# A written-out order for all five queues, new from the first gated attention to the first channel mixing

## The chip, the core and the metric

The kernel runs on one core of a Trainium2 chip. The metric is the device time of one launch in microseconds (us), lower is better; of several runs of one kernel the median counts. Five engines work in parallel, each through a queue of its own in the order in which the queue is written: PE (TensorE), DVE (VectorE), ACT (ScalarE), POOL (GpSimd) and SP (SyncE, which here only issues DMAs). An instruction that needs another engine's result waits on a semaphore, and all that stands behind it in the same queue waits too.

## What is computed

Three layers follow each other, on two batch entries of 768 positions:

```python
x = concat_heads(banded_attention(q, k, v))     # 8 heads of 64; 31-wide band and 24 block summaries
for e in range(4):                              # gated attention: 4 experts, the 2 best are weighted per position
    q, k, v = x @ wq[e], x @ wk[e], x @ wv[e]
    a = softmax(causal(q @ k.T / 8))
    out += gate[:, e] * (a @ v @ wo[e])
u = out + (relu(out.T @ w_tok1) @ w_tok2).T     # token mixing
y = u + relu(u @ w_ch1) @ w_ch2                 # channel mixing, 512 -> 1536 -> 512
```

The top-2 gate is a softmax over the two largest of four logits. The matrices of the mixings arrive as 64-bit floats and are decoded on the chip.

## The kernel before

Almost every product runs as three matmuls of the rounded fp32r type (`mm3`, lines 112 to 114): each operand is kept as a high part, which ACT writes, and a remainder, which DVE subtracts (`split`, lines 104 and 105), so each matmul result costs one ACT and one DVE pass before it can be multiplied again.

The stages, with the names that the rows use (b is the batch entry, e the expert, h the half of 384 positions):

- `s1`, the banded attention (lines 217 to 282); its tiles begin with s1, and sm, ri, pr.
- `proj`: pv (values and gate logits, b and block) and pj (queries and keys). Their split copies are moved by SP's DMAs into q2, k2 and k2l.
- `attn`, the gated attention: for each of 4 experts and 2 halves, PE makes the scores s2s (line 476: queries by keys, then by the keys' remainder) in a PSUM bank of the group "sc"; DVE masks and takes the row minimum of the negated scores (line 481, tiles pr and mn); ACT takes the exponential (line 486, which adds up sm); POOL adds a small constant (488); DVE inverts (489, tile f); POOL scales pr by f and the gate, three blocks of rows (492); PE turns pr in 128x128 blocks (502, bank s2p); ACT copies the turned block (104: ph, 506: pf), DVE makes the remainder (105: pl); PE multiplies by the values into s2a (507, 512, 513); ACT and DVE join the halves (516: tmp, 517: yT). The digits after s2s, s2p, s2a are b, e, h and then the bank. Half h = 0 has row blocks of 128, 256 and 384 keys, half h = 1 of 512, 640 and 768.
- `tokmix`, with tiles yh, yl, yt (turn, 535), nh, nl, z, g and u; `chmix`, with h and o, in four passes over 384 hidden columns.
- `decode_w` (lines 138 to 153): per 128x512 weights ACT 143 and 149, POOL 144, 150, 151 and 153, DVE 145 to 147, ACT 152. Tiles raw and deca; t1, t2, c1, c2 are the decoded weights.

The stages overlap: generators of the stages are interleaved by shares (`run`), so the first gated attention shares its time with `proj` of batch 1 and the decoding of the token weights, and the second with the token mixing of batch 0 and the first channel pass. `run` gives only the order in which the program is traced. What stands in the queues is chosen by the framework's scheduler from that, with its own estimates of durations; only the first banded attention (`FIRST`) is fixed by hand. PSUM has eight banks in three groups (sc 3, pt 3, acc 2), so a matmul that opens a bank also waits for the last reader of the bank's former tile.

Of the kernel before, what the change touches and what calls it, by code (L numbers as in the profile page):

```python
# [790 lines left out]
```

## Time and profile before

| | us |
|---|---|
| median of 3 runs | 466.64 |
| lowest, highest | 465.47, 469.15 |
| profiled execution, its own time | 467.73 |
| span of its instructions | 465.9 |
| PE busy in the span | 445.1 (96%) |

The rows further down come from the profiled execution. A row of the timeline gives the start (us from the span's start), the length, the engine, the line of the kernel, the operation, what it writes and reads, its shape, how many were merged, and in square brackets the idle time before it with the instruction that ended it. A PE matmul's length contains its way through the array, so neighbours overlap; what one costs is the distance to the next one's start.

### The profile page before, as it was taken

To read this page: it belongs to the slowest core of one execution; us is meant where nothing else is said; L and a number is where in the kernel's file an instruction comes from. 1 tells how busy PE (TensorE), PEld (TensorE's weight loads), DVE (VectorE), ACT (ScalarE), POOL (GpSimd) and SP (SyncE) were. 2 spreads that over 40 slices of the span, in tenths; PEclk is the share of its full clock that TensorE was granted. 3 is DMA by queue.
4 is the path that set the end of the run, shared out by engine and by line. 5 is a ranking of instruction groups with operands and counts; after the bars stand their busy time and mean duration, and the time that the engine had idled before them with its cause. 6 is when DMAs were issued, how large, how long until landed. Compare 5 with 4: busy or idle time off the path is not lost.

```text
span 465.9 us, 8565 instructions
## 1 busy us (share of the span) xinstructions
PE 445.1 (96%) x3038; PEld 420.7 (90%) x3038; DVE 280.1 (60%) x818; ACT 231.2 (50%) x653; POOL 285.2 (61%) x319
## 2 busy tenths in 40 slices
PE   7899899999989878999999999999999999999996
PEld 7798789989978766897999999999999999999996
DVE  5573766759699679868773743677572673332322
ACT  4685665977778687885664423233323321111010
POOL 4568542768989887997873869877864771000000
PEclk9999999999999999999999999999999999999999
DMA  7999917806515865021111120212121100001111
GB/s 222 275 255 310 289 39 207 182 2 167 127 46 152 210 171 146 3 91 45 45 47 46 66 70 2 84 53 78 58 91 45 62 32 0 1 0 69 68 70 68
DMA packets 28522, 46.51 MB, mean 100 GB/s; under 512 B 2496, under 2 KB 19648, under 8 KB 28480
## 3 DMA queue, kind: packets, MB, share of 16 engines
q1 hardware_dynamic: 28480, 45.97, 35.2%
q8 instruction: 24, 0.39, 0.4%
q14 instruction: 18, 0.15, 0.1%
HBM read 33.38 MB, written 3.15 MB: 78 GB/s over the span
## 4 chain that ended last, share of the span: by engine, by line
PE 68%; DMA 10%; DVE 7%; POOL 4%; ACT 3%; issue 3%; SPq 3%; DVEq 0%; ACTq 0%; POOLq 0%
PE h L113 7%; PE h L112 7%; PE h L114 7%; PE o L112 7%; PE o L113 7%; PE o L114 7%; DMA kx<-in_kwT_dram 5%; PE s1s L217 4%; PE s1a L271 2%; DMA qb<-in_qT_dram 2%; POOL pr L492 2%; PE u L112 2%; PE pj L112 2%; PE u L113 2%; PE u L114 2%
## 5 line engine op out<-in xcount | busy, mean ns | idle before, releaser
L144 POOL TENSOR_SCALAR deca<-deca 128x512 f32<-128x512 f32 x30 | 58.0, 1938 | 10.5 <-ACT deca L143 9.7
L113 PE MATMUL o<-hl,c2h 128*128 128x384 f32 x192 | 64.2, 337 | 0.0
L114 PE MATMUL o<-hh,c2l 128*128 128x384 f32 x192 | 64.0, 336 | 0.0
L108 ACT ACTIVATE hh<-h 128x384 fp32r<-128x384 f32 x48 | 23.3, 490 | 79.4 <-PE h L114 78.8
L109 DVE SCALAR_TENSOR_TENSOR hl<-h,hh 128x384 fp32r<-128x384 f32 x48 | 26.5, 555 | 53.2 <-ACT hh L108 53.2
L605 DVE TENSOR_TENSOR oa<-o,oa 128x384 f32<-128x384 f32 x64 | 31.9, 550 | 38.5 <-PE o L114 38.5
L112 PE MATMUL o<-hh,c2h 128*128 128x384 f32 x192 | 49.4, 336 | 0.0
L236 ACT ACTIVATE pr<-n,mn 128x120 f32<-128x120 f32 x96 | 36.6, 384 | 16.3 <-DVE mn L227 15.8
L150 POOL TENSOR_TENSOR raw<-raw 128x512 f32<-128x512 f32 x30 | 31.3, 1042 | 20.4 <-DVE raw L147 18.6
L492 POOL TENSOR_SCALAR pr<-pr,f,wg 128x128 f32<-128x128 f32 (+5 forms) x48 | 40.1, 849 | 5.1 <-DVE f L489 2.9
L151 POOL TENSOR_TENSOR deca<-deca,raw 128x512 f32<-128x512 f32 x30 | 40.8, 1360 | 1.0
L149 ACT ACTIVATE raw<-raw 128x512 f32<-128x512 uint32 x30 | 20.3, 677 | 36.3 <-DMA raw<-in_ch_dram 25.6
L145 DVE TENSOR_SCALAR deca<-deca 128x512 int32<-128x512 int32 x30 | 27.8, 928 | 14.9 <-POOL deca L144 14.9
L486 ACT ACTIVATE pr<-pr,mn 128x128 f32<-128x128 f32 (+5 forms) x48 | 31.9, 665 | 9.8 <-DVE mn L481 9.7
L113 PEld LDWEIGHTS o<-hl,c2h 128*128 128x128 f32 x192 | 36.0, 188 | 0.3 <-DVE hl L109 0.3
L114 PEld LDWEIGHTS o<-hh,c2l 128*128 128x128 f32 x192 | 36.0, 188 | 0.0
L112 PEld LDWEIGHTS o<-hh,c2h 128*128 128x128 f32 x192 | 34.8, 188 | 0.1
L113 PE MATMUL h<-u0l,c1h 128*128 128x384 f32 x96 | 32.5, 338 | 0.0
L112 PE MATMUL h<-u0h,c1h 128*128 128x384 f32 x96 | 32.4, 338 | 0.0
L114 PE MATMUL h<-u0h,c1l 128*128 128x384 f32 x96 | 32.3, 337 | 0.0
L112 PE MATMUL h<-u1h,c1h 128*128 128x384 f32 x96 | 32.3, 336 | 0.0
L113 PE MATMUL h<-u1l,c1h 128*128 128x384 f32 x96 | 32.3, 336 | 0.0
(207 smaller groups left out, 1315.1 us busy)
## 6 DMA issues: line engine op xcount, KB each, us to landing
raw<-in_ch_dram SPq DMA_DIRECT2D x24, 512.0 KB, 3.5
kx<-in_kwT_dram SPq DMA_DIRECT2D x7, 720.0 KB, 10.0
vx<-in_vw_dram SPq DMA_DIRECT2D x8, 576.0 KB, 11.1
qb<-in_qT_dram SPq DMA_DIRECT2D x16, 192.0 KB, 8.9
raw<-in_tok_dram SPq DMA_DIRECT2D x6, 512.0 KB, 4.6
out_dram<-oa SPq DMA_DIRECT2D x16, 192.0 KB, 2.0
vt<-in_vT_dram SPq DMA_DIRECT2D x4, 384.0 KB, 10.3
rqk<-in_wqkv_dram SPq DMA_DIRECT2D x4, 256.0 KB, 10.2
```

The lines of the kernel that those rows point to most:

```text
L109: vec.scalar_tensor_tensor(lo, src, 0.0, hi.bitcast(F32), op0=ALU.max, op1=ALU.subtract)
L112: ten.matmul(out, lh, rh, start=start, stop=False)
L113: ten.matmul(out, lh, rl, start=False, stop=False)
L114: ten.matmul(out, ll, rh, start=False, stop=stop)
L144: gps.tensor_scalar(af, af, F64_TINY, F64_HUGE, op0=ALU.max, op1=ALU.min)
L145: vec.tensor_scalar(ta, ta, 3, 0x3FFFFFFF, op0=ALU.logical_shift_left, op1=ALU.bitwise_and)
L150: gps.tensor_mul(lf, lf, ef)
L151: gps.tensor_add(af, af, lf)
L236: act.activation(pr[:, i, :], n[:, i, :], AF.Exp, bias=mn[:, i:i + 1], scale=-1.0, accum_out=sm[:, i:i + 1])
L486: act.activation(prs[r], prs[r], AF.Exp, bias=mn[:, r, ci:ci + 1], scale=-1.0, accum_out=sm[:, r:r + 1])
L492: gps.tensor_scalar(prs[r][:, :nk], prs[r][:, :nk], f[:, r:r + 1], wg[:, 3 * h + r, e:e + 1], op0=ALU.mult, op1=ALU.mult)
L605: vec.tensor_add(oa[d], a[:, :HALF], oa[d])
```

## The change

A table `ORDER` is added, with one line of positions for each of the five queues: it names, for each place in the queue, the traced instruction that stands there. At the end of the program a chain of dependencies without semaphores is laid along each line, so the scheduler has nothing left to choose:

```diff
+ORDER = {
+    "PE": """
+0-192 253-257 193-216 258-262 281-284 298 263-264 299-301 217-236 265 269-277 306-314 330-331 285 266 237-252 267-268
...
+    queues = {"PE": ten, "DVE": vec, "ACT": act, "POOL": gps, "SP": nc.sync}
+    traced = list(nc.cur_bb.bb.instructions)
+    for name, table in ORDER.items():
+        mine = [x for x in traced if x.engine == queues[name].engine and type(x).__name__.startswith("Inst")]
+        places = []
+        for run_ in table.split():
+            a, _, z = run_.partition("-")
+            places += range(int(a), int(z or a) + 1)
+        assert sorted(places) == list(range(len(mine))), (name, len(places), len(mine))
+        for a, z in zip(places, places[1:]):
+            tc.add_manual_dep(mine[z], mine[a].name, NOSYNC, reason="keep_in_program_order")
```

No instruction is added, dropped or resized. Ahead of the 506th PE instruction (88 us of the trace before) and from the 1742nd on (299 us) the queues are those of before. Between them other places hold 1138 of 2673 PE instructions, 352 of 818 on DVE, 251 of 508 on ACT, 128 of 315 on POOL and 29 of 142 DMA issues of SP. The table stands ahead of the code, so line numbers after the change are higher by 104 (L580 is L476 of before, L606 is L502, and so on).

**Place 1, ACT at the end of the first gated attention.** pf is the copy of a turned block that PE multiplies next; pf_2527 stands 14 rows behind pf_2500 in before. Its first rows (pr768_2633 is of batch 1, expert 0, second half; the pr of 2749 to 2751 of batch 1, expert 1, first half):

```order
L506 ACTIVATE pf_2500<-s2p0310_2496 128x384
L486 ACTIVATE pr768_2633,sm2_2629<-pr768_2633,mn2_2628 128x768
L104 ACTIVATE ph_2507<-s2p0311_2503 128x384
L486 ACTIVATE pr128_2749,sm2_2747<-pr128_2749,mn2_2746 128x128
L143 ACTIVATE deca_2734<-raw64_2733 128x512
L149 ACTIVATE raw64_2733<-raw64_2733 128x512
L486 ACTIVATE pr256_2750,sm2_2747<-pr256_2750,mn2_2746 128x256
L104 ACTIVATE s111h_2394<-pj1111_2439 128x384
L104 ACTIVATE ph_2517<-s2p0312_2513 128x384
L516 ACTIVATE tmp_2436<-s2a030_2411 64x384
L143 ACTIVATE deca_2813<-raw64_2812 128x512
L149 ACTIVATE raw64_2812<-raw64_2812 128x512
```

The rows from pf_2500 on now, where pf_2527 is nine rows behind it:

```order
L610 ACTIVATE pf_2500<-s2p0310_2496 128x384
L256 ACTIVATE t2h_2140<-deca_2273 128x2x256
L208 ACTIVATE ph_2507<-s2p0311_2503 128x384
L590 ACTIVATE pr256_2563,sm2_2560<-pr256_2563,mn2_2559 128x256
L590 ACTIVATE pr128_2562,sm2_2560<-pr128_2562,mn2_2559 128x128
L208 ACTIVATE s111h_2394<-pj1111_2439 128x384
L208 ACTIVATE ph_2517<-s2p0312_2513 128x384
L620 ACTIVATE tmp_2436<-s2a030_2411 64x384
L208 ACTIVATE yh0_2584<-yT0_1526 128x768
L610 ACTIVATE pf_2527<-s2p0313_2523 128x384
L208 ACTIVATE ph_2533<-s2p0314_2530 128x256
L208 ACTIVATE ph_2541<-s2p0315_2539 128x128
```

The two decoding pairs (deca and raw64) and the exponentials pr768_2633, pr128_2749, pr256_2750 and pr384_2751 of batch 1 stood between pf_2500 and pf_2527; now they stand behind pf_2527, and two exponentials of batch 1, expert 0, first half, are left between the two.

**Place 2, PE in the first gated attention, second half of expert 0.** Scores s2s011x of expert 1, and turns s2p001x of expert 0. Before:

```order
L502 MATMUL s2p0010_1750<-ident_76,pr512_1678 128x128
L502 MATMUL s2p0011_1757<-ident_76,pr512_1678 128x128
L502 MATMUL s2p0012_1767<-ident_76,pr512_1678 128x128
L476 MATMUL s2s0112_1929<-k200_1070,q200_1069 128x512
L476 MATMUL s2s0112_1929<-k2l00_1071,q200_1069 128x512
L502 MATMUL s2p0010_1750<-ident_76,pr640_1679 128x128
L502 MATMUL s2p0011_1757<-ident_76,pr640_1679 128x128
L502 MATMUL s2p0012_1767<-ident_76,pr640_1679 128x128
L476 MATMUL s2s0113_1934<-k200_1070,q200_1069 128x512
L476 MATMUL s2s0113_1934<-k2l00_1071,q200_1069 128x512
L502 MATMUL s2p0010_1750<-ident_76,pr768_1680 128x128
L502 MATMUL s2p0011_1757<-ident_76,pr768_1680 128x128
```

Now:

```order
L580 MATMUL s2s0112_1929<-k200_1070,q200_1069 128x512
L580 MATMUL s2s0112_1929<-k2l00_1071,q200_1069 128x512
L580 MATMUL s2s0113_1934<-k200_1070,q200_1069 128x512
L580 MATMUL s2s0113_1934<-k2l00_1071,q200_1069 128x512
L216 MATMUL pj1000_1968<-x1h0_717,wqk0h_111 128x384
L217 MATMUL pj1000_1968<-x1l0_719,wqk0h_111 128x384
L218 MATMUL pj1000_1968<-x1h0_717,wqk0l_112 128x384
L216 MATMUL pj1000_1968<-x1h0_717,wqk0h_111 128x384
L217 MATMUL pj1000_1968<-x1l0_719,wqk0h_111 128x384
L218 MATMUL pj1000_1968<-x1h0_717,wqk0l_112 128x384
L606 MATMUL s2p0010_1750<-ident_76,pr512_1678 128x128
L606 MATMUL s2p0010_1750<-ident_76,pr640_1679 128x128
```

The groups of three turns that stood between the score banks are taken out; the banks follow each other directly, then half of projection pj1000, and the turns come as nine in a row.

**Place 3, PE and DVE at the start of the second gated attention.** The last score bank of batch 1, expert 0, second half (s2s1013) and what follows it on PE. Before, where 75 instructions stand between it and the first turn of the same half, s2p1010:

```order
L476 MATMUL s2s1013_2651<-k210_1964,q210_1963 128x512
L476 MATMUL s2s1013_2651<-k2l10_1965,q210_1963 128x512
L513 MATMUL s2a021_2285<-pl_2332,V01_758 128x128
L502 MATMUL s2p0301_2419<-ident_76,pr256_2373 128x128
L502 MATMUL s2p0301_2419<-ident_76,pr384_2374 128x128
L535 MATMUL yt02_2724<-ident_76,yT0_1526 128x128
L507 MATMUL s2a030_2411<-pf_2416,V01_758 128x384
L502 MATMUL s2p0302_2428<-ident_76,pr384_2374 128x128
L502 MATMUL s2p0310_2496<-ident_76,pr512_2465 128x128
L502 MATMUL s2p0310_2496<-ident_76,pr640_2466 128x128
L502 MATMUL s2p0310_2496<-ident_76,pr768_2467 128x128
L512 MATMUL s2a030_2411<-ph_2422,V01_758 128x256
```

Now; behind the last row shown stand ten more instructions (one s2a031, one s2p1002, two s2s1101, two yt01, four s2a100), and then s2p1010:

```order
L580 MATMUL s2s1013_2651<-k210_1964,q210_1963 128x512
L580 MATMUL s2s1013_2651<-k2l10_1965,q210_1963 128x512
L606 MATMUL s2p1001_2601<-ident_76,pr256_2563 128x128
L606 MATMUL s2p1001_2601<-ident_76,pr384_2564 128x128
L617 MATMUL s2a031_2495<-pl_2534,V01_758 128x256
L616 MATMUL s2a031_2495<-ph_2541,V01_758 128x128
L639 MATMUL yt02_2724<-ident_76,yT0_1526 128x128 x2
L616 MATMUL s2a100_2590<-ph_2595,V10_1572 128x384
L580 MATMUL s2s1100_2752<-k210_1964,q210_1963 128x128
L580 MATMUL s2s1100_2752<-k2l10_1965,q210_1963 128x128
L580 MATMUL s2s1100_2752<-k210_1964,q210_1963 128x256
L580 MATMUL s2s1100_2752<-k2l10_1965,q210_1963 128x256
```

On DVE, from the last row minimum of the same half (pr768_2633) to the reciprocal f2_2630 that its scaling needs. Before:

```order
L481 ISA pr768_2633,mn2_2628<-s2s1013_2651,cmask_80,mn2_2628 128x512
L481 ISA mn2_2628 128x1
L517 TENSOR_TENSOR yT0_1526<-s2a021_2285,tmp_2337 64x384
L126 TENSOR_TENSOR wol_2341<-rw512_2346,woh_2340 128x512
L105 TENSOR_TENSOR pl_2423<-s2p0301_2419,ph_2422 128x256
L105 TENSOR_TENSOR pl_2431<-s2p0302_2428,ph_2430 128x128
L481 ISA pr128_2749,mn2_2746<-s2s1100_2752,cmask_80 128x128
L481 ISA mn2_2746 128x1
L481 ISA pr256_2750,mn2_2746<-s2s1100_2752,cmask_80 128x256
L481 ISA mn2_2746 128x1
L489 RECIPROCAL f2_2630<-sm2_2629 128x3
```

Now:

```order
L585 ISA pr768_2633,mn2_2628<-s2s1013_2651,cmask_80,mn2_2628 128x512
L585 ISA mn2_2628 128x1
L249 TENSOR_SCALAR deca_2734<-deca_2734 128x512
L209 TENSOR_TENSOR pl_2542<-s2p0315_2539,ph_2541 128x128
L230 TENSOR_TENSOR wol_2341<-rw512_2346,woh_2340 128x512
L585 ISA pr128_2749,mn2_2746<-s2s1100_2752,cmask_80 128x128
L585 ISA mn2_2746 128x1
L585 ISA pr256_2750,mn2_2746<-s2s1100_2752,cmask_80 128x256
L585 ISA mn2_2746 128x1
L250 SCALAR_TENSOR_TENSOR deca_2734<-raw64_2733,deca_2734 128x512
L593 RECIPROCAL f2_2630<-sm2_2629 128x3
```

Counted in PE instructions, s2s1013 has moved back by 47 places and s2p1010 has come forward by 7, so 21 instructions are left between the two. On DVE two steps of a weight's decoding (L249 and L250, of before L145 and L146) now stand between the row minimum and the reciprocal.

## Rows read from the trace of the kernel before

**Rows 1.** Windows: us, busy time (instructions) by engine, clock, DMA.

```profile
84.00:120.00 36.00, 36.00 (x325) 32.95 (x325) 25.25 (x108) 30.78 (x102) 27.55 (x45) 1.00 0.51 121
120.00:152.00 32.00, 30.14 (x186) 26.45 (x184) 27.17 (x86) 24.00 (x64) 29.64 (x31) 1.00 0.36 97
152.00:178.00 26.00, 22.07 (x131) 18.29 (x132) 19.82 (x55) 19.25 (x52) 21.69 (x25) 1.00 0.79 191
178.00:240.00 62.00, 58.47 (x359) 51.68 (x358) 50.19 (x127) 45.88 (x111) 53.39 (x50) 1.00 0.19 60
240.00:460.00 220.00, 220.00 (x1272) 219.14 (x1272) 103.86 (x172) 59.30 (x114) 107.26 (x82) 1.00 0.14 47
```

**Rows 2.** Waits of PE, 84 to 250 us: total, times, longest.

```profile
PE s2a L507 <- ACT pf L506: 1.8, 2, 1.3
...
PE s2s L476 <- DVE mn L481: 0.8, 2, 0.6
PE s2s L476 <- issue: 0.6, 1, 0.6
PE s2s L476 <- DMA k2l<-s101l: 0.6, 1, 0.6
...
PE yt L535 <- DVE yT L517: 0.3, 1, 0.3
```

**Rows 3.** Timeline of PE around one wait, 181.8 to 183.7 us.

```profile
181.89 0.42 PE L512 MATMUL s2a<-ph,V 128*128 128x384 f32 x1
183.17 0.38 PE L112 MATMUL z<-t1h,nh 128*128 128x256 f32 x1 [0.86 <-DVE mn L481]
183.40 0.28 PE L113 MATMUL z<-t1l,nh 128*128 128x256 f32 x1
```

**Rows 4.** Timeline of ACT, from pf_2500 to pf_2527 (place 1).

```profile
163.94 0.50 ACT L506 ACTIVATE pf<-s2p 128x384 f32<-128x384 f32 x1
...
167.14 0.70 ACT L143 ACTIVATE deca<-raw 128x512 f32<-128x512 f32 x1 [0.62 <-DMA raw<-in_ch_dram]
...
172.64 0.47 ACT L506 ACTIVATE pf<-s2p 128x384 f32<-128x384 f32 x1
```

**Rows 5.** Timeline of PE and DVE, 114.5 to 116.2 us (place 2).

```profile
114.54 0.69 DVE L481 CUSTOM_DVE_ANT_0 pr<-s2s,cmask 128x512 f32<-128x512 f32 x1 [0.68 <-PE s2s L476]
...
114.81 0.49 PE L502 MATMUL s2p<-ident,pr 128*128 128x128 f32 x3
...
115.30 0.50 PE L476 MATMUL s2s<-k,q 128*128 128x512 f32 x1
...
116.07 0.74 DVE L481 CUSTOM_DVE_ANT_0 pr<-s2s,cmask,mn 128x512 f32<-128x512 f32 x1
```

**Rows 6.** Timeline of four engines, 161.6 to 178 us: s2s1013 to s2p1010 (place 3).

```profile
161.64 0.40 PE L476 MATMUL s2s<-k2l,q 128*128 128x512 f32 x1
...
163.43 0.72 DVE L481 CUSTOM_DVE_ANT_0 pr<-s2s,cmask,mn 128x512 f32<-128x512 f32 x1
...
164.31 0.95 ACT L486 ACTIVATE pr<-pr,mn 128x768 f32<-128x768 f32 x1
...
166.38 0.20 POOL L488 TENSOR_SCALAR sm<-sm 128x3 f32<-128x3 f32 x1
...
166.61 0.18 DVE L489 RECIPROCAL f<-sm 128x3 f32<-128x3 f32 x1 [0.32 <-POOL sm L488]
...
166.96 2.60 POOL L492 TENSOR_SCALAR pr<-pr,f,wg 128x512 f32<-128x512 f32 x3 [0.38 <-DVE f L489]
...
177.93 0.51 PE L502 MATMUL s2p<-ident,pr 128*128 128x128 f32 x3
```

**Rows 7.** Groups of DVE, 100 to 240 us, shapes apart: count, busy us, mean ns.

```profile
L146 DVE SCALAR_TENSOR_TENSOR deca<-raw,deca 128x512 int32<-128x512 int32 x14 | 12.2, 869 | 0.1
L145 DVE TENSOR_SCALAR deca<-deca 128x512 int32<-128x512 int32 x14 | 10.1, 721 | 2.8 <-POOL deca L144 2.8
```

**Rows 8.** POOL's scaling by line: count, duration ns least/median/most.

```profile
L492 POOL TENSOR_SCALAR pr<-pr,f,wg x48: 442/876/1699, 98.1 to 230.6; 128x128 f32<-128x128 f32 x8, 128x256 f32<-128x256 f32 x8, 128x384 f32<-128x384 f32 x8, 128x512 f32<-128x512 f32 x8
```

More of the change, by code (lines that the diff above doesn't have):

```diff
@@ new lines @@
+903-904 943 938 968-970 941 946-948 972-974 949-951 977-979 982-984 952-957 986-987 942 944-945 971 975-976 990
+980-981 1011-1018 985 988 999-1001 1019-1022 1004-1005 989 991 1051-1052 1002 1053-1056 992 1008 1057-1058 1023-1024
+1003 1006-1007 1009 1025-1027 1075-1080 1030-1032 1010 1035-1037 1081-1084 1028 1085-1086 1029 1033 1040-1042
+1131-1136 1044-1045 1137-1139 1061-1062 1034 1038 1048 1149-1152 1059-1060 1039 1043 1153-1154 1179-1184 1046
+1191-1192 1047 1049-1050 1063-1065 1068-1069 1193-1196 1072 1066 1140-1148 1087-1092 1197-1198 1093-1104 1199-1200
@@ new lines @@
+1105-1107 1110-1112 1067 1070-1071 1239-1241 1073 1115-1117 1074 1108 1242-1244 1109 1120-1122 1113 1124-1125 1114
+1118 1251-1252 1128 1253-1254 1155-1160 1255-1256 1119 1123 1161-1163 1293-1295 1164-1169 1172-1173 1176 1126
+1296-1301 1245-1247 1185-1187 1127 1170 1248-1250 1129 1188-1190 1130 1201-1203 1171 1174 1305-1306 1302-1304
+1307-1310 1175 1177-1178 1204-1209 1213-1215 1218-1220 1311-1314 1216 1269-1271 1223-1225 1228-1230 1217 1221-1222
+1272-1274 1210-1212 1226 1275-1277 1232-1233 1227 1236 1278-1280 1353-1355 1257-1268 1281-1283 1356-1364 1286-1287
@@ new lines @@
+1290 1231 1234-1235 1237-1238 1367-1375 1284 1315-1326 1285 1327-1329 1332-1334 1288-1289 1291-1292 1330 1337-1339
+1376-1378 1342-1344 1331 1335-1336 1346-1347 1340 1379-1382 1341 1345 1350 1365-1366 1383-1388 1348-1349 1351-1352
+1389-1391 1399-1404 1392-1394 1397-1398 1422-1424 1395-1396 1411-1412 1425-1427 1405-1407 1413-1415 1440-1442
+1458-1463 1416-1418 1443-1445 1428-1439 1446-1457 1467-1469 1500-1502 1473-1475 1479-1484 1503-1505 1470-1472
+1488-1490 1476-1478 1408-1410 1512-1514 1491-1493 1515-1517 1521-1523 1533-1535 1464-1466 1524-1526 1485-1487
@@ new lines @@
+2296-2297 2304-2305 2280 2289 2298 2306 2281-2282 2290-2291 2299-2300 2307-2308 2283 2292 2301 2309 2284-2285
+2293-2294 2302-2303 2310-2349 2358 2367 2350-2351 2359-2360 2368-2369 2376-2377 2352 2361 2370 2378 2353-2354
+2362-2363 2371-2372 2379-2380 2355 2364 2373 2381 2356-2357 2365-2366 2374-2375 2382-2421 2430 2439 2422-2423
+2431-2432 2440-2441 2448-2449 2424 2433 2442 2450 2425-2426 2434-2435 2443-2444 2451-2452 2427 2436 2445 2453
+2428-2429 2437-2438 2446-2447 2454-2493 2502 2511 2494-2495 2503-2504 2512-2513 2520-2521 2496 2505 2514 2522
@@ new lines @@
+2497-2498 2506-2507 2515-2516 2523-2524 2499 2508 2517 2525 2500-2501 2509-2510 2518-2519 2526-2565 2574 2583
+2566-2567 2575-2576 2584-2585 2592-2593 2568 2577 2586 2594 2569-2570 2578-2579 2587-2588 2595-2596 2571 2580 2589
+2597 2572-2573 2581-2582 2590-2591 2598-2637 2646 2655 2638-2639 2647-2648 2656-2657 2664-2665 2640 2649 2658 2666
+2641-2642 2650-2651 2659-2660 2667-2668 2643 2652 2661 2669 2644-2645 2653-2654 2662-2663 2670-2672
+""",
+    "DVE": """
+0-84 94-95 85-87 115 96-99 114 116 88-89 103-104 108-112 120 129 133 121-124 113 90 125 91 138 92-93 100 105 101-102
@@ new lines @@
+590 622 591 625-627 592-598 602-603 607-608 612-614 618-619 623-624 628-657
+""",
+    "ACT": """
+0-69 76-79 84-87 70-73 91-94 88 74-75 80 82 95 81 83 89 96 98 90 104-105 97 100-101 99 102-103 106 112-114 108-110 107
+111 116 115 117 122 118-120 123 121 124 129 125-127 130 128 131 136 132-133 137 134-135 138-143 145-147 144 155 151
+154 150 148-149 152 159 158 153 156 160-161 170 162 157 169 171-172 165 164 163 166 180 173 181 174 176-177 167-168
+214 225 215 178 184 175 183 226 182 185 179 186-188 216 198-199 201 200 209 231-232 202 211 189-191 227 192-193 210
@@ new lines @@
+350-351 374 372 371 352-353 349 375 354 365 376 360 355 364 385 413 366-367 356 414 368 377-379 373 369 380-382
+390-391 383 389 418 388 384 419 387 394 392 422 393 396-398 415 420-421 426 425 399-400 395 404 423 431 403 402 430
+401 434 405 407 406 409 444 408 410 427 432 411 433 443 412 416-417 435 449 448 445 424 428 452 451 429 450 456 455
+436 453 437 461 460 438 457 464 463 439 462 440 474 441 473 465 442 478-479 446-447 482 486 454 458 475 480 459 481
+485 466-467 483 468 491 490 487 494 493 469-470 492 471 495 472 476-477 484 488-489 496-507
@@ new lines @@
+""",
+    "POOL": """
+0 2 1 3-41 48 50 56-57 63 49 42 64 51 43-46 52-55 58 47 59-62 65 70 66-69 71-92 96 93-94 102 95 97 99-101 98 103-104
+107 105 108 106 112 111 110 109 113-114 116 115 129 133 130-131 117 134 132 118 120 119 121 135 123 122 141 136 125
+124 128 127 142 126 145 143 137 140 138 146 139 144 153 147 154-156 149 148 163 157 165-166 164 150 167 151 169-170
+152 158 168 159 161 160 171-172 174 162 173 179 175-176 178 177 183 180 184 186 181 187 185 182 191 195 193 192 188
+199 194 189 202 201 190 200 207 196-197 203 210 209 198 215 204 211 205 216 208 206 217-218 212 219 213 223 214 225
@@ new lines @@
+224 220 239 226 221-222 240-241 243 230 228-229 227 244-245 242 246-247 255-257 248-250 259 233 232 234 260 236 261
+235 231 237 251 238 252-253 258 262-263 254 267 264-265 268 266 269 271 270 275 272-273 276 274 277 279 278 283
+280-281 284 282 285 287 286 288 291 289-290 292 295 293 296-297 294 298-299 303 300-301 304 302 305 307 306 311
+308-309 312 310 313-314
+""",
+    "SP": """
+0-35 39 70 75 37-38 36 40-58 60 59 61 76 62 67 69 63-66 68 77 86-87 73 71 74 72 78 80-81 84-85 83 90 79 91 93 88 92 82
@@ L49 @@
+89 102 95 94 96 100 99 97 101 98 103-141
+""",
+}
 F64_TINY = 2.0 ** -15
```

44 lines of the change are left out of this document (added).

## The prediction

> **What bounds the kernel now.** I began with the table of windows. PE has no idle time from 84 to 120 us and none from 240 to 460 us, where it is busy 220.00 of 220 us; it is idle 1.86 us between 120 and 152, 3.93 between 152 and 178 and 3.53 between 178 and 240, 9.32 us in all [rows 1]. That is the stretch in which the queues change. The clock is granted in full (1.00) in each window, so PE's time falls only where it stops standing. In none of the three windows is another engine full: POOL, the busiest, works 29.64 of 32, 21.69 of 26 and 53.39 of 62 us, DVE 27.17, 19.82 and 50.19 [rows 1]. PE waits for latency there, not for an engine without time to spare, and latency is something that an order can cover.
>
> The list of PE's waits comes next. It has 18 waits in 16 rows; the largest row, for ACT's copy pf, has 1.8 us in two waits, one of 1.3, and most of the others are single waits between 0.3 and 0.9 us, ended by DVE, ACT or a DMA [rows 2, 3]. A wait costs more than its idle time. Around one of 0.86 us the start of the matmul ahead and the start of the waiting one lie 183.17 - 181.89 = 1.28 us apart [rows 3], where 384 columns otherwise take 220 / 1272 = 0.17 [rows 1]: 0.25 us are lost beside the idle time. I take 0.2 for each, 3.6 us for 18. So 9.3 + 3.6 = 12.9 us is all that the new order can win. What is won stays won: PE has no gap behind 240 us, POOL, which decodes the weights that are still to come, works 107 of the last 220 us [rows 1], and the queues behind 299 us are the old ones.
>
> **The change part by part.** Nothing is added, removed or resized, so busy times hardly change; the sum is one of waits that go and waits that come.
>
> Place 1, the end of the first gated attention, holds the longest wait (1.3 us for pf [rows 2]). ACT reached that copy at 172.64, 8.7 us after the copy pf_2500 at 163.94 [rows 4]. Between the two it did two pairs of decoding steps (the first, of 0.70 us, after 0.62 us of waiting for a DMA [rows 4]) and four exponentials of batch 1, none of which PE needed yet. They now stand behind the copy, so it comes some 4 us sooner against the rest of ACT's work, and PE has six score matmuls of batch 1 to do ahead of it. This wait goes. The two waits of 0.6 us at the first scores of batch 1, one of them for a DMA of k2l [rows 2], go as well: those scores now stand behind the rest of a projection, some 4 to 5 us of PE work later, and the SP issues, of which 29 change places, stay ahead of them.
>
> Place 3 pays for it. The scores of batch 1's first halves moved back, the turns that need their softmax did not. Before, the last scores of expert 0's second half ended at about 161.9 and their first turn came at 177.93, while POOL had scaled the last block at 166.96 + 2.60 = 169.56 [rows 6]: 8.4 us of reserve. Now 21 instructions are left between: 7 turns, and 4 matmuls of 384, 5 of 256 and 5 of 128 columns. At 0.16 us for a turn (three in 0.49 [rows 5]) and 0.17 us for 384 columns, less in proportion for fewer, that is 2.7 us. A matmul behind one of another kind costs more than its columns (0.23 us for the first of 256 columns in rows 3, against 0.12), so I use 3.0. The chain that they must cover is row minimum 0.72, exponential 0.95, sum 0.20, reciprocal 0.18 and three scalings 2.60: 4.65 us with every queue empty; as it ran, 169.56 - 161.9 = 7.7 us [rows 6]. In DVE's queue two decoding steps, 0.72 and 0.87 us [rows 7], now stand between minimum and reciprocal, so the lower end is not to be had: with them the chain is 6.2 us, and I take 6.7, between that and the time it took. PE then waits 6.7 - 3.0 = 3.7 us ahead of s2p1010 (bounds 4.65 - 3.0 = 1.6 and 7.7 - 2.7 = 5.0). Behind that turn in PE's queue stand the scores of the next half and the first values of batch 1; they all slip with it. So the window from 152 to 178 us, with 3.93 us idle now, wins 0.2.
>
> POOL's part of that chain is the least certain. The same line takes from 442 to 1699 ns, with a median of 876 [rows 8], and not by columns alone: the three of rows 6, with 512, 640 and 768 columns the largest there are, took 0.87 on the mean. [...]
>
> Place 2 adds waits where there were none. Three turns (0.49 us at 114.81) stood ahead of the score bank at 115.30, which cannot open before DVE's minimum, begun at 114.54, ends at 115.23 [rows 5]. Without them PE stands from 114.81: 0.45 us. Two banks of twice 0.23 us (512 columns) then end at about 116.2, and the projection behind them needs the bank whose minimum ends at 116.07 + 0.74 = 116.81 [rows 5]: 0.55 us more. That is 1.0 us; nothing if DVE comes sooner by its own new order, at most 1.5 if a remainder is still queued ahead of the minima.
>
> The other 11 waits, 1.86 + 3.53 = 5.39 us [rows 1], I did not follow one by one. For each I compared how far its two ends moved, in summed durations, on their own engines. By that count all but one (0.6 us, scores waiting for a minimum) lose their idle time, because the producer moved ahead by more than PE's waiting instruction. But the same count also clears the whole window of place 3, where following the chain put 3.7 of 3.93 us back. So I let half of it return: 2.7 us won. The ends are 4.8 and nothing.
>
> With fewer places to wait, 18 may become 10: 8 x 0.2 = 1.6 us won. The sum is 0.2 - 1.0 + 2.7 + 1.6 = 3.5 us. The profiled execution took 467.73 us (span 465.9 and 1.8 around it) and would take 464.2. It lies 1.1 us above the median of the runs, 466.64; from that, 463.1.
>
> **The rivals.**
> 1. The order covers what it sets out to cover. Place 3 costs its lower bound of 1.6, place 2 its 1.0, both with a restart (0.6 for three), and all other waits but one go: 12.9 - 0.8 - 1.6 - 1.0 - 0.6 = 8.9 us won, 457.7 us. For it: no engine is full in the stretch [rows 1] and the waits are many and short [rows 2]. Against it: the 21 instructions and the two decoding steps of place 3.
> 2. The idle time only moves. Each wait that goes turns up behind the next product, because DVE and ACT now wait for PE where PE waited for them: 466.6 us. For it: place 3, where that comes out almost to the microsecond. Against it: PE stood still for just the instructions that now have more in front of them.
> 3. Slower, by place 3 alone. If the decoding step in front of the reciprocal waits for POOL's own part of that decoding, as it did for 2.8 us in sum [rows 7], and the scalings take their longest time (2.5 us more [rows 8]), the chain becomes 6.7 + 2.8 + 2.5 = 12.0 us and the wait 9.0, 5.1 more than the window has now. With place 2's 1.0 and nothing won elsewhere that is 472.7 us. It decides from a wait of about 8 us at s2p1010, if little is won elsewhere.
> [...]
>
> **How the numbers follow.** The forecast, 463.1 us, gets 0.42, with a range of its own from 460.5 to 466. Rival 1 gets 0.36, rival 2 0.11, rival 3 0.09 and rival 4 0.02. A measurement of this kernel can tell about 1% from no change, that is 462.0 and 471.3 us. Faster than that are rival 1 and a seventh of the forecast, 0.42. Rivals 3 and 4 are slower by more than that, 0.11. The rest, 0.47, is no change that can be told. The range from 456.5 to 468.5 takes in rivals 1 and 2 and leaves out the other two; its lower end lies 1.2 us under rival 1, for place 2 costing nothing.
>
> **What would show it.** In the profile after, the wait for pf and the two waits at batch 1's first scores should be gone; PE's list of waits should be headed by turns s2p at the start of the second gated attention, released by POOL's pr, with 2 to 5 us; two short waits of scores or projection on DVE's minima should stand near 115 us; PE idle from 84 to 240 us should be 6 to 8 us instead of 9.3, with the clock still 1.00, and full from there on. I am wrong if no wait of a turn on POOL's pr is over 1.5 us (then rival 1), if the idle sum is still 9 us (rival 2), or if that wait is over 8 us (rival 3).

## The result and the profile after

The changed kernel takes 468.84 us (median of 20 runs, 465.25 to 471.29) where before takes 466.12 (20 runs, 464.29 to 471.56). The ratio is 1.0052, with a 95% interval of 1.0028 to 1.0075: slower by 2.4 us, where the forecast of 463.1 was a gain of 3.5, and just above the range, which ends at 468.5. The profiled execution has a span of 468.1 us against 465.9. Ratios and intervals, here and below, leave out executions in a slower state, among them the profiled one of e1 (a mean clock of 0.56), so the waits of e1 are not read.

The table of windows of after, columns as in [rows 1]:

```profile
84.00:120.00 36.00, 34.42 (x305) 30.08 (x305) 23.30 (x102) 28.07 (x96) 23.46 (x42) 1.00 0.37 93
120.00:152.00 32.00, 31.03 (x193) 27.57 (x193) 25.41 (x84) 25.30 (x66) 28.33 (x31) 1.00 0.45 115
152.00:178.00 26.00, 23.21 (x139) 19.30 (x138) 21.20 (x54) 19.43 (x50) 19.24 (x22) 1.00 0.81 192
178.00:240.00 62.00, 58.87 (x363) 53.36 (x363) 51.31 (x131) 47.48 (x117) 56.92 (x53) 0.97 0.19 61
240.00:460.00 220.00, 219.52 (x1269) 218.41 (x1268) 108.57 (x179) 60.97 (x117) 113.17 (x86) 1.00 0.15 50
```

Read the first and the last row first. Where before had no idle time PE now stands 1.58 us (84 to 120) and 0.48 us (240 to 460); the three windows between went from 1.86, 3.93 and 3.53 to 0.97, 2.79 and 3.13. The sum is 8.95 us, against 9.32. (After runs up to 5.5 us late here, so a window does not hold quite the same instructions in both.) And one window has a clock of 0.97, where before has 1.00. Finer windows of after show where:

```profile
170.00:175.00 5.00, 4.88 (x30) 3.78 (x28) 4.24 (x13) 3.24 (x9) 1.67 (x3) 1.00 1.04 262
175.00:180.00 5.00, 2.05 (x10) 1.36 (x11) 4.11 (x16) 4.63 (x17) 2.48 (x4) 1.00 0.83 221
180.00:185.00 5.00, 4.97 (x26) 4.31 (x27) 3.73 (x11) 3.86 (x8) 4.43 (x7) 0.66 0.03 10
```

At place 3 PE works 2.05 of 5 us, and behind that the clock record has 3.41 us at a share of 0.5 (from 180.76 us). In that time a score matmul of 512 columns takes 0.42 us to the next one's start (at 182.62), where it takes 0.23 at a clock of 1.00 (at 117.80). If all of PE's work takes twice as long there, half of the 3.41 us is lost, 1.7: an estimate from these two records, and its upper end. In before no such record stands there:

```profile
170.00:175.00 5.00, 3.68 (x19) 2.60 (x19) 4.22 (x9) 4.57 (x12) 4.10 (x4) 1.00 0.89 204
175.00:180.00 5.00, 4.28 (x24) 3.06 (x23) 4.94 (x15) 3.06 (x8) 4.12 (x5) 1.00 0.52 112
180.00:185.00 5.00, 4.14 (x30) 3.40 (x29) 5.00 (x14) 4.22 (x9) 4.41 (x4) 1.00 0.43 125
```

The list of PE's waits of after, 84 to 305 us (total, times, longest):

```profile
PE yt L639 <- DVE pl L209: 1.5, 1, 1.5
PE s2s L580 <- DVE mn L585: 1.5, 3, 0.7
PE s2p L606 <- POOL pr L596: 1.2, 2, 0.8
PE s1a L375 <- DVE x1l L386: 0.9, 1, 0.9
...
PE o L216 <- DVE hl L213: 0.3, 1, 0.3
PE s1p L361 <- POOL pr L356: 0.3, 1, 0.3
```

The wait for pf, which headed [rows 2], and the two at batch 1's first scores are gone. The list is headed by a turn of the token mixing (yt) that waits for a remainder (pl) on DVE. The rows s1a and s1p lie in the head, the row o behind 240 us, where before had no wait.

### The profile page after: what moved, and what is told of

It is laid out like the page before. It is cut to its first block, busy times and chain, and to the rows that moved or that the text cites. A ratio compares the mean times of both kernels' runs of the same rounds, so it can differ in the third digit from the quotient of the medians.

```text
span 468.1 us, 8553 instructions
## 1 busy us (share of the span) xinstructions
PE 448.7 (96%) x3038; PEld 424.5 (91%) x3038; DVE 282.7 (60%) x818; ACT 232.5 (50%) x653; POOL 286.1 (61%) x319
## 4 chain that ended last, share of the span: by engine, by line
PE 69%; DMA 9%; POOL 8%; DVE 7%; SPq 3%; ACT 2%; issue 2%; DVEq 0%; POOLq 0%; ACTq 0%
PE o L216 7%; PE h L218 7%; PE h L217 7%; PE o L217 7%; PE h L216 7%; PE o L218 7%; DMA kx<-in_kwT_dram 3%; PE s1s L321 3%; PE s2s L580 2%; PE s1a L375 2%; PE s2p L606 2%; POOL pr L596 2%; PE u L216 2%; PE u L217 2%; PE u L218 2%
## 5 line engine op out<-in xcount | busy, mean ns | idle before, releaser
L216 PE MATMUL o<-hh,c2h 128*128 128x384 f32 x192 | 51.0, 336 | 0.3 <-DVE hl L213 0.3
L596 POOL TENSOR_SCALAR pr<-pr,f,wg 128x128 f32<-128x128 f32 (+5 forms) x48 | 38.6, 812 | 4.0 <-DVE f L593 2.4
L249 DVE TENSOR_SCALAR deca<-deca 128x512 int32<-128x512 int32 x30 | 25.7, 858 | 12.9 <-POOL deca L248 12.9
L218 PE MATMUL h<-u1h,c1l 128*128 128x384 f32 x96 | 32.3, 336 | 0.0
```

Of the source, the lines that this page charges most:

```text
L216: ten.matmul(out, lh, rh, start=start, stop=False)
L218: ten.matmul(out, ll, rh, start=False, stop=stop)
L249: vec.tensor_scalar(ta, ta, 3, 0x3FFFFFFF, op0=ALU.logical_shift_left, op1=ALU.bitwise_and)
L596: gps.tensor_scalar(prs[r][:, :nk], prs[r][:, :nk], f[:, r:r + 1], wg[:, 3 * h + r, e:e + 1], op0=ALU.mult, op1=ALU.mult)
```

## Where the time went, position by position

Ahead of PE's 506th instruction the queues are the same, and at the 690th, 760th, 910th, 1060th, 1330th and 1750th nearly the same instructions stand behind PE in both orders (three at most are exchanged). So the start of PE's n-th instruction can be set beside its start in before. The 500th and the 690th (counted from 0), first in before, then in after:

```profile
87.15 0.28 PE L217 MATMUL s1s<-kx,qb 128*128 128x120 f32 x1
112.91 0.28 PE L113 MATMUL pv<-wvl,x1h 128*128 128x260 f32 x1
...
88.17 0.28 PE L321 MATMUL s1s<-kx,qb 128*128 128x120 f32 x1
116.61 0.29 PE L217 MATMUL pv<-wvl,x1h 128*128 128x260 f32 x1
```

After is 1.02 us late at the one and 3.70 at the other, so between the two it lost 2.7 us. Counting from the 500th leaves out what the unchanged first part does from run to run. All runs below are read in this way; spare instructions (e5, e6, e9, e14, e16) are counted out.

| us lost (+) or won (-) | 500 to 690, head | 690 to 760, place 2 | 760 to 910 | 910 to 1060, place 3 | 1060 to 1330 | 1330 to 1750 | to the end | sum | ratio, 95% |
|---|---|---|---|---|---|---|---|---|---|
| after | +2.7 | +1.8 | -2.0 | +0.1 | -2.5 | +1.3 | -0.2 | +1.2 | 1.0052 (1.0028 to 1.0075) |
| e2 new head | +2.7 | +4.8 | -1.7 | -0.2 | +0.4 | 0.0 | -0.2 | +5.8 | 1.014 (1.009 to 1.019) |
| e3 old head | -0.1 | +1.0 | -2.0 | -0.8 | -2.4 | +1.3 | -0.2 | -3.2 | 0.9955 (0.9925 to 0.9986) |
| e4 new middle | -0.1 | +0.1 | +0.1 | -0.8 | -2.5 | +7.4 | +0.3 | +4.5 | 1.0137 (1.0099 to 1.0176) |
| e5 e3, matmuls | -0.1 | +1.0 | -1.9 | -1.7 | -2.2 | +1.4 | -0.2 | -3.8 | 0.9939 (0.9903 to 0.9974) |
| e6 e3, turns | -0.1 | +1.0 | -2.0 | -1.3 | -2.1 | +1.4 | -0.2 | -3.3 | 0.9919 (0.9888 to 0.9949) |
| e7 old to 760 | -0.1 | 0.0 | -2.0 | -0.4 | -2.5 | +1.3 | -0.2 | -3.8 | 0.993 (0.9901 to 0.9959) |
| e8 eased | -0.1 | +1.0 | -1.9 | +0.3 | -2.6 | +1.3 | -0.2 | -2.2 | 0.9934 (0.9902 to 0.9966) |
| e9 after, matmuls | +2.7 | +2.1 | -1.9 | -1.6 | -2.3 | +1.3 | -0.2 | +0.1 | 1.0009 (0.9987 to 1.003) |
| e10 relieved | -0.1 | 0.0 | -1.9 | +2.3 | -2.0 | +1.4 | -0.2 | -0.6 | 0.9987 (0.9963 to 1.0012) |
| e11 old place 3 | -0.1 | +0.1 | -0.9 | +3.7 | -3.5 | +1.3 | -0.2 | +0.3 | 1.001 (0.9987 to 1.0033) |
| e12 one copy | +2.1 | +2.5 | -2.0 | -0.6 | -2.5 | +1.3 | -0.2 | +0.6 | one execution |
| e13 relieved, b | -0.1 | +0.1 | -2.0 | -0.7 | -2.1 | +1.3 | -0.2 | -3.6 | 0.9913 (0.9884 to 0.9942) |
| e14 e7, turns | -0.1 | 0.0 | -2.0 | -1.4 | -2.2 | +1.3 | -0.2 | -4.6 | 0.9927 (0.9898 to 0.9957) |
| e15 tail | -0.1 | +0.1 | -2.0 | +0.2 | -2.4 | +0.6 | -0.2 | -3.9 | 0.9902 (0.9866 to 0.9938) |
| e16 tail, turns | -0.1 | +0.1 | -2.0 | -1.4 | -2.1 | +0.6 | -0.2 | -5.1 | 0.9879 (0.9859 to 0.9899) |

Where no edit and no joint lies in them or just ahead, most columns hold still: the head costs 2.7 us wherever the new order stands in it, 760 to 910 wins 2.0 and 1060 to 1330 some 2.5 (2.0 to 2.6 behind the edits of place 3). Two columns do not. Place 2 costs 1.0 us behind the old head and 1.8 to 2.5 behind the new one (after, e9, e12), where PE's list of waits has 0.4 us for a DMA of k2l (after) or 0.8 and 0.7 for ACT's pf (e9, e12). And place 3 differs from run to run.

## The experiments

**e1 to e4: stretches of the two orders.** The table allows mixtures. A queue gives first what had started by a position in the trace of the one kernel, in that kernel's order, then the rest in the other's. The diff of e3 against after, at PE's place of the longest wait in the head:

```diff
-L375 MATMUL s1a_1457<-pTs,vx_948 64x64 x8
-L361 MATMUL s1p_1449<-ident,pr 120x128 x4
-L361 MATMUL s1p_1474<-ident,pr 120x128 x4
+L361 MATMUL s1p_1474<-ident,pr 120x128 x2
+L580 MATMUL s2s_1686<-k_1070,q_1069 128x128
...
 L375 MATMUL s1a_1482<-pTs,vx_1186 64x64 x8
```

- e1: 

> The order of before, written as a table for all five queues: no instruction changes its place. Theory (the loss sits in new places of the order): 466.1 us, the median of before, within 1 us, no wait of 1 us or more on PE between 84 and 240 us that before did not have. Rival (fixing the order by a table costs time by itself): near after's 468.8 us.


- e2: 

> The new order only up to PE's 690th instruction (113 us in before, 117 in after), before's order behind it. Position by position, after's PE is 1.0 us late at the 506th instruction, where the orders part, and 3.7 us late at the 690th. Theory (the head, where before had no idle time, carries the loss): 466.1 + 2.7 = 468.8 us. [...]


- e3: 

> Before's order up to PE's 690th instruction, the new order behind it: the change with its head undone. Theory (head carries the loss): 468.8 - 2.7 = 466.1 us, as before, since behind the head after loses about as much to the clock at 181 us and to waits as it wins at 186 to 226 us. Rival (clock and place 3 carry the loss): 468.8 us, with the clock at 0.5 for 3 us near 180 us again.


- e4: 

> The new order only from PE's 910th to its 1330th instruction (151 to 230 us in before), before's order ahead of it and behind it. [...] Rival (idle time only moves: the waits that go here turn up behind it): 466.1 us.

e1 came to 0.9997 (0.9967 to 1.0028): a table by itself costs nothing that shows. e3 took 465.80 us (before 467.42 on the same chip): the change without its head is faster than before. Of the 4.5 us or so by which its sum is below after's, 2.8 are the head, 0.8 place 2 behind it and 0.9 place 3. e2 shows the same 2.7 us in the head, and e4 wins 2.5 us from 1060 to 1330 and 0.8 at place 3, where after wins 2.4 in all (+0.1 and -2.5); but both came out far slower than these stretches add up to, by their joints (e2 has one wait of 1.9 us there, and its profile a mean clock of 0.986). Behind e4's joint PE stood once for 5.0 us:

```profile
PE s2a L614 <- ACT ph L206: 5.0, 1, 5.0
```

At that joint POOL's queue stood three instructions behind where the old order has it, and ACT, ahead of that copy, stood 2.20 us for POOL's step of a decoding and then 3.01 us for a DMA of raw weights. The clock fell at 237.4 us for 6.83 us (a mean of 0.977 in this profile). So a sum of stretches holds only where nothing is owed at the joint.

**e5, e6 and e9: the clock.** In e3's profile the clock's record at 0.5 begins at 175.56 us, right behind waits of 0.69 us (s2s1101) and 1.55 us (yt01), and lasts 3.41 us. The edit of e5; e6 has `ten.transpose(pT[:, HALF:], ident, ident)` in its place, and e9 puts e5's into after:

```diff
                         ten.transpose(pT[:, P * r:P * r + P], prs[r][:, P * j:P * j + P], ident)
+                    if b == 1 and e == 0 and h == 0 and j == 2:
+                        for _ in range(18):
+                            ten.matmul(pT[:, HALF:], k2[0][:, 0, :P], q2[0][:, 0, :P], start=True, stop=True)
```

- e5: 

> e3 (before's order up to PE's 690th instruction, then the new one) with 18 spare matmuls of 128 columns put into two waits of PE at the start of the second gated attention: 6 ahead of s2s1101 (0.69 us of waiting in e3) and 12 ahead of yt01 (1.55 us). They write an unused quarter of a PSUM bank, so the program computes the same and waits for the same. [...] Theory (idle time of PE makes the clock fall): the fall between 165 and 185 us is gone, and up to 1.7 us with it, 464 us beside e3's 465.8. Rival (the fall has nothing to do with the waits): the fall stays, 465.8 us.


- e6: 

> As e5, but the 18 spare instructions are turns of 128 columns (matmuls in transpose mode) in the same two places. [...] Rival (turns are work as any other): it goes as in e5, 464 us.


- e9: 

> The changed kernel itself, with the 18 spare matmuls of e5 in the same two waits of place 3 and nothing else changed. Theory (of after's loss the fall of the clock behind place 3 is up to 1.7 us and the head the rest): after stands at 1.0052 of before; without the fall it comes to 466.1 + 2.7 - 1.7 = 467.1 us beside before's 466.1 (a ratio of 1.002), with the head's idle time of 1.2 us still there. Rival (the clock explains the whole loss): 1.000 or less. Rival (the head explains the whole loss): 1.005.

Windows of e6, to be set beside after's (e6 is some 4 us ahead of after here):

```profile
170.00:175.00 5.00, 4.49 (x31) 3.56 (x30) 4.48 (x17) 4.75 (x14) 2.43 (x3) 1.00 0.90 210
175.00:180.00 5.00, 4.58 (x35) 3.81 (x32) 4.61 (x15) 4.58 (x11) 4.30 (x6) 1.00 0.26 89
180.00:185.00 5.00, 4.59 (x33) 4.03 (x32) 4.59 (x17) 4.65 (x12) 4.91 (x6) 1.00 0.29 91
```

In all three profiles the fall at place 3 is gone (a clock of 1.00 from 160 to 190 us), and the mean clock over all runs tells the same: 0.986 in e3, 0.989 and 0.990 in e7 and e8 (the same chip as e5 and e6), against 0.995 and 0.994 in e5 and e6; 0.990 in after, 0.995 in e9. So the fall at place 3 came with the idle time there, and 18 instructions in its place keep the clock at 1.00. The turns did it as well as the matmuls (a mean clock of 0.994 in e6, 0.995 in e5), as the rival of e6 has it. e9 is 0.0043 below after, 2.0 us; its interval holds its theory's 1.002 and the first rival's 1.000 and leaves out the 1.005 of the second. Its place 3 wins 1.6 us where after loses 0.1; e5 and e6 won less, 0.9 and 0.4, and their ratios cannot be told from e3's. In the next stretch 0.2 to 0.3 us of this goes again. All the same the clock is not the whole: e9 only draws level with before, since the head's 2.7 us are still in it.

**e7: place 2.** Diff against e3 (nine turns go back between the score banks; three of them shown). The rest of the stretch goes back with them: 74 places on PE differ in all, 18 on DVE, 13 on ACT, 9 on POOL and 6 on SP.

```diff
+L606 MATMUL s2p_1750<-ident,pr_1678 128x128
+L606 MATMUL s2p_1757<-ident,pr_1678 128x128
+L606 MATMUL s2p_1767<-ident,pr_1678 128x128
 L580 MATMUL s2s_1929<-k_1070,q_1069 128x512
```

- 

> Before's order up to PE's 760th instruction (124 us in before), the new order behind it: e3 with place 2 undone as well. In e3 PE lost 1.1 us between the 690th and the 730th instruction (place 2) and was 1.0 us later than in before at the 760th. Theory (place 2 costs its 1.0 us): 465.8 - 1.0 = 464.8 us, no wait of PE near 115 us. Rival (it is given back before 150 us, where the new order has idle time to spare): 465.8 us.

Place 2 goes from +1.0 to 0.0 and nothing behind it takes that back except place 3 (-0.8 to -0.4, where one execution differs from another by as much): 463.75 us. By positions the theory holds, for the stretch and not for the nine turns alone; the ratios of e3 and e7 cannot be told apart.

**e12: the longest wait of the head.** The timeline of after shows what held the bank of s1a for 0.91 us:

```profile
98.28 0.60 ACT L366 ACTIVATE pTs<-s1p 120x512 f32<-120x512 f32 x1 [1.32 <-PE s1p L361]
...
98.77 0.38 ACT L383 ACTIVATE x1h<-s1a 128x256 fp32r<-128x256 f32 x1
...
99.18 0.42 DVE L386 TENSOR_TENSOR x1l<-s1a,x1h 128x256 fp32r<-128x256 f32 x1 [1.17 <-ACT x1h L383]
...
99.66 0.34 PE L375 MATMUL s1a<-pTs,vx 120*64 120x64 f32 x4 [0.91 <-DVE x1l L386]
```

ACT stands 1.32 us for PE's turns before pTs; the copy x1h, whose bank had long been written, waits behind it, and DVE and PE wait for x1h. The edit, on ACT, in after:

```diff
+L383 ACTIVATE x1h_718<-s1a_1415 128x256
 L366 ACTIVATE pTs<-s1p_1449 120x512
-L383 ACTIVATE x1h_718<-s1a_1415 128x256
```

- 

> The changed kernel with one instruction moved by one place: on ACT the copy x1h1 of bank s1a121 stands ahead of the copy pTs_1454, not behind it. In after, pTs_1454 waited 1.32 us for PE's turns, x1h1 behind it ended at 99.15 and DVE's remainder at 99.61, and PE stood 0.91 us at s1a130, which opens the bank that they read. Theory (that place in ACT's queue makes the wait): the wait at s1a130 is gone or under 0.2 us, and PE's loss against before from its 506th to its 600th instruction falls from 2.6 to 1.4 us. Rival (the eight turns in a row leave too little work ahead of s1a130 anyway): the wait stays over 0.6 us.

The wait is 0.18 us now, but the head's loss only falls from 2.7 to 2.1, and at the 760th instruction nothing is left of that (4.6 us lost, 4.5 in after): 0.7 us at a turn that waits for ACT's pf has come in, a wait that e9 has too (0.8), without this edit. The cause of the wait at s1a is shown; that it was the price of the head is not. PE's list has 1.2 us of waits in the head of after (0.9 here, 0.3 at s1p for POOL), so more than half of the 2.7 us is no idle time in the trace but starts that lie further apart. What sets them apart was not tried.

**e8, e10, e13 and e11: place 3.** In after DVE's queue, ahead of the remainder that PE's yt waits for:

```profile
175.95 0.43 DVE L249 TENSOR_SCALAR deca<-deca 128x512 int32<-128x512 int32 x1 [0.89 <-POOL deca L248]
...
176.49 0.68 DVE L230 TENSOR_TENSOR wol<-rw,woh 128x512 fp32r<-128x512 f32 x1
...
177.65 0.72 DVE L250 SCALAR_TENSOR_TENSOR deca<-raw,deca 128x512 int32<-128x512 int32 x1
...
179.26 0.55 DVE L209 TENSOR_TENSOR pl<-s2p,ph 128x384 fp32r<-128x384 f32 x1
```

And the scalings on POOL, with the first turn of s2p1010 on PE:

```profile
178.63 2.60 POOL L596 TENSOR_SCALAR pr<-pr,f,wg 128x512 f32<-128x512 f32 x3 [0.80 <-DVE f L593]
...
180.82 0.42 PE L606 MATMUL s2p<-ident,pr 128*128 128x128 f32 x1
```

In e7, beside which e10, e11 and e13 are set, PE stands idle for 2.56 us from 165 to 180 us, and the clock's record at 0.5 lasts 3.41 us there. e8 moves the remainders (its PE edit is that of s2p1010 behind four scores), e10 and e13 the decoding too; the DVE part of e13, which is e10's without the move of L230:

```diff
-L249 TENSOR_SCALAR deca<-deca 128x512
 L209 TENSOR_TENSOR pl<-s2p_2539,ph 128x128
...
-L250 SCALAR_TENSOR_TENSOR deca<-raw_2733,deca 128x512
+L209 TENSOR_TENSOR pl<-s2p_2591,ph 128x384
...
 L209 TENSOR_TENSOR nl_2622<-yt_2661,nh_2621 128x256
+L249 TENSOR_SCALAR deca<-deca 128x512
+L250 SCALAR_TENSOR_TENSOR deca<-raw_2733,deca 128x512
```

- e8: 

> e3 with place 3 eased: on DVE the remainders pl_2542, pl_2596 and pl_2605 stand ahead of a step of a weight's decoding and of two remainders of the token mixing; on PE the three turns s2p1010 stand behind two transposes yt05 and four score matmuls. Theory (the long wait of place 3 is DVE's queue, and it brings the clock down): the wait of 1.55 us at yt01 goes, at most 0.5 us of it turns up at s2a100 or s2p1010, and the fall near 176 us goes with it: 1.0 + 1.7 = 2.7 us, 463.1 us. Rival (PE then waits for POOL's scaled blocks instead): a wait of over 1 us at s2p1010, 465 to 466 us.


- e10: 

> e7 (before's order up to PE's 760th instruction, then the new one) with work taken off DVE in place 3: the two decoding steps and the remainder of a weight (L249, L250, L230; 1.8 us together) stand behind the last remainder nl0 instead of between the minima, the remainders pl_2542, pl_2596, pl_2605 and ACT's copy ph_2604 come sooner, and the turns s2p1010 stand behind four score matmuls as in e8. In e8 the wait of 1.55 us only moved to the next score bank (1.24 us), with DVE busy 4.5 of 5 us. [...] Rival (the chain over ACT and POOL is as long as DVE's queue): idle time stays near 2.5 us and the fall with it, 463.8 us.


- e13: 

> e10 with the remainder wol_2341 (L230) back in its place on DVE. In e10 the DMA of the next raw weights waited for wol_2341 (issued at 174.50, after its end at 174.44), ACT stood 4.37 us for that DMA at deca_2813, and the copy ph_2671 behind it held PE for 2.35 us. Theory (with the DMA in time again the relief of DVE works): DMA issued near 170 us, no wait of PE for ph_2671, idle time between PE's 910th and 1060th instruction 2 us against 3.5 in e7, no fall of the clock between 165 and 190 us: 463.8 - 1.5 - 1.7, so 460.5 to 462 us. Rival (another wait takes its place once more, since ACT, DVE and POOL are each busy over 4 of 5 us there): 463.5 us or more, with a fall.


- e11: 

> e7 with place 3 undone too: before's order also between PE's 910th and 1060th instruction. Theory (place 3's new order wins 0.4 us of waiting there and pays up to 1.7 us for the clock): no fall between 165 and 190 us, idle time of 4.3 us there as in before instead of 3.5, and 463.8 + 0.4 to 0.8 - 1.7, so 462 to 463 us. Rival (before's waits there bring the clock down as well, only elsewhere): 464 us or more. The two joints, where the queues of DVE and POOL differ by four and three instructions, can add a wait of about 1 us each.

The theory of e8 fell: yt no longer waits for pl, but a score bank stands 1.24 us for the minimum that now comes later on DVE, and the clock falls for 6.83 us (0.95, 0.50 and 0.87 in the three windows from 170 to 185 us). e10 came out slower than e7 (0.9987 beside 0.993), by a wait that I had not followed. ACT in e10:

```profile
173.08 0.84 ACT L208 ACTIVATE yh<-yT 128x768 fp32r<-128x768 f32 x1 [0.22 <-DVE yT L621]
178.30 0.67 ACT L247 ACTIVATE deca<-raw 128x512 f32<-128x512 f32 x1 [4.37 <-DMA raw<-in_ch_dram]
```

The DMA of the next raw weights needs the buffer that wol (L230) reads, and with L230 moved back it was issued at 174.50 instead of 170.44 us (e7); PE stood 2.35 us for a copy behind it in ACT's queue. e13 mends that, and its clock stays up, as its windows show:

```profile
170.00:175.00 5.00, 4.01 (x25) 2.88 (x23) 4.54 (x18) 4.06 (x9) 1.92 (x1) 1.00 1.03 234
175.00:180.00 5.00, 3.71 (x20) 2.50 (x20) 4.20 (x12) 4.73 (x15) 2.98 (x5) 1.00 0.55 137
180.00:185.00 5.00, 3.70 (x25) 3.08 (x25) 5.00 (x16) 3.57 (x9) 4.52 (x5) 1.00 0.01 2
```

PE has more idle time between its 910th and 1060th instruction than in e7 (4.69 us against 3.54), but in ten waits of at most 0.73 us, and no fall. That comes out even: -0.7 against -0.4 at place 3. So the rival of e13 has it for PE's idle time and for the time, 463.58 us (a ratio of 0.9913 beside e7's 0.993), though the fall that it named did not come. e11 tells nothing on the price of place 3: at its joint PE waits 3.4 us for a DMA of keys, and the clock falls with that wait (0.83 from 150 to 160 us); at place 3 itself, in before's order, it does not fall (1.00 from 160 to 190 us).

**e14 to e16: do the parts add up.** e15's edit on DVE, and the same once more for hl_3929:

```diff
+L213 SCALAR_TENSOR_TENSOR hl<-h_3498,hh 128x384
 L250 SCALAR_TENSOR_TENSOR deca<-raw_3949,deca 128x512
 L209 TENSOR_TENSOR nl_3460<-yt_3520,nh_3459 128x256
-L213 SCALAR_TENSOR_TENSOR hl<-h_3498,hh 128x384
```

- e14: 

> e7 (before's order up to PE's 760th instruction, then the new one) with the 18 spare turns of e6 in the two waits of place 3. Theory (the parts add up): e7's ratio of 0.993 less 1 to 1.7 us for the clock, so 0.990, 461.5 to 462.5 us where before has 466.1 to 467.5; no fall between 165 and 190 us. Rival (the spare turns cost as much as the clock gives back): 0.993, as e7.


- e15: 

> e7 (before's order up to PE's 760th instruction, then the new one) with two instructions moved on DVE behind the second gated attention: the remainders hl_3512 and hl_3929 stand ahead of a decoding step (L250) instead of behind it. In e7 PE loses 1.3 us to before between its 1330th and 1750th instruction, with waits of 0.3 and 0.2 us at o0001 and o1003 for these two. Theory (the two places in DVE's queue make that loss): 0.8 us of the 1.3 come back, the two waits are gone, 463.8 - 0.8 = 463.0 us. Rival (only half of the loss is theirs, or another remainder is late next): 0.4 us or less come back.


- e16: 

> e15 with the 18 spare turns of e14 in the two waits of place 3. Beside e15 on the same chip it shows what the spare turns give. Theory (a fall of the clock there costs 1 us net, since PE has waits behind it that take up a part): e15's time less 0.8 to 1.0 us, 462 us, a ratio of 0.989 to before. Rival (they give nothing): as e15.

e14 is at 0.9927 beside e7's 0.993: by the ratio its rival holds, by positions it wins 1.0 us at place 3 and gives 0.3 of that back in the next stretch. e15's two waits are gone and 0.7 of 1.3 us come back, as its theory says. e16 has the lowest ratio of all: 461.18 us where before took 466.93 on the same chip, ahead of both kernels. Its place 3 wins 1.6 us more than e15's (-1.4 against +0.2). The intervals of e15 and e16 overlap, so what the spare instructions give at place 3 is shown by positions in five pairs (0.4 to 1.7 us), each of two single executions, and by the ratio only between after and e9.

## Why the prediction was wrong

- The windows. "PE has no idle time from 84 to 120 us" was read as if nothing could be lost there but place 2. This is the step that failed: the sum has no term for the head, and it measures 2.7 us lost, with 0.8 more behind it at place 2. A full stretch says that every wait is covered, not by how much. I compared reserve and chain at place 3 alone; the same comparison at s1a would have shown its longest wait coming: between the turns s1p_1449, which ACT waits for ahead of the copy x1h, and s1a_1482 stood 28 instructions on PE, and now stand four. What makes up the rest of the 2.7 us stays open (e12).
- "What is won stays won" failed for the same reason: behind the 1330th instruction 1.3 us are lost, 0.7 of them to two remainders behind decoding steps (e15).
- Place 2: 1.0 us forecast, 1.0 measured (e3 against e7), with a wait of a score bank for DVE's minimum as forecast (0.33 us of idle time in e3, the rest beside it). Right; the 1.8 us of after have the late head in them.
- Place 1: right, the wait went, and so did the two at batch 1's first scores.
- Place 3: 0.2 us won forecast, 0.1 lost. That the size came so near was luck: less waiting than forecast and a fall of the clock that was not forecast make it up. The longest wait is ended by DVE's pl at yt, 1.55 us, not by POOL's pr at s2p1010, and no wait of a turn on POOL's pr is over 0.8 us, where the prediction called itself wrong below 1.5. The decoding steps in DVE's queue, which I counted against the reciprocal, hold up the remainder first. The chain was nearly as long as forecast, 7.1 us against 6.7 (from the last scores' end at 174.1 us to 181.23), but the waits of 0.72, 0.69 and 1.55 us ahead of s2p1010 had covered it by then. POOL's three scalings took 2.6 us as before, so the 2.5 us more that rival 3 gives them did not come into it.
- The other waits and restarts: 2.7 + 1.6 = 4.3 us won forecast; 2.0 + 2.5 = 4.5 measured (760 to 910, 1060 to 1330), of which 2.4 are idle time. The sum is right, but it was a guess at half.
- The clock "granted in full, so PE's time falls only where it stops standing": failed. Between PE's 910th and 1060th instruction its idle time fell from 5.2 to 4.5 us, and the stretch still lost 0.1, since the clock was at 0.5 for 3.41 us of it. The spare matmuls give back 1.7 us there by positions, 2.0 by the ratios. Rival 4, a fall of the clock, had a chance of 0.02: the fall came at place 3, where spare turns in the waits keep the clock at 1.00 (e6), and none stands behind the nine turns of place 2 (1.00 from 120 to 152 us).
- The sum, then: 0.2 - 1.0 + 4.3 = 3.5 won forecast; in the profile 4.5 won and 2.7 + 1.8 + 0.1 + 1.3 - 0.2 = 5.7 lost. Rival 2 (the idle time only moves) comes nearest, with 8.95 of 9.32 us left. Rival 3's price did not come, though its first half is in the trace: DVE's decoding step waited 0.89 us for POOL. The ratio's 2.4 us (1.3 to 3.5 by its interval) are more than the profile's 1.2, which is one execution set beside another; why is not shown.

## What to carry to other kernels

A stretch without idle time has reserves, and a new order spends them unseen: for each bank or copy that an engine waits for, compare the work left ahead of the waiting instruction with the chain that it waits for, in the full stretches too. One long wait can cost as much as several short ones of a larger sum (e7, with 3.54 us of idle time, a longest wait of 1.6 and a fall of 3.41 us, has -0.4 at place 3; e13, with 4.69 us in waits of at most 0.73 and no fall, has -0.7), by what the clock does behind it. Before an instruction is moved back on a full engine, ask which DMA waits for the buffer that it frees.

## What was not expected of the hardware

- At place 3 the clock's record at 0.5 lasts 3.41 us in after, e3 and e7 and 6.83 us in e8. It stands behind waits that lie together (0.72, 0.69 and 1.55 us within some 5 us in after), and there is none behind the ten waits of up to 0.73 us of e13, although their sum is larger than e7's (4.69 against 3.54 us).
- Falls of the clock also come near 12 and 48 us, in the part that all kernels share, in some executions and not in others (6.83 us from 47.64 us in after; 0.83 from 10 to 20 us, 0.96 and 0.87 in the two windows from 40 to 60 in e3; 1.00 up to 460 us in before), and with its waits for DMAs that part ends between 4.2 us sooner and 3.5 us later than in before's profile. How much of the scatter of single runs comes from there was not measured.
- The decoding step L250 takes 0.72 us at place 3 in after and 1.39 at 237.34 us in e7. With hl_3512 ahead of it, it takes 0.68 in e15, and L251 behind it 1.22 instead of 0.63. Of its 30 in after's trace the 13 long ones (0.83 to 1.69 us) all run beside an instruction of POOL, and the five with none beside them took 0.68 to 0.69; but 12 more ran beside POOL and took no longer than 0.72. What decides was not tried.
